# Attention ahead of a Sinkhorn-routed MoE on one core: another order of TensorE's pieces in the attention

## The chip, the cores and the metric

One Trainium2 chip, one of its cores. The metric is device time in microseconds of one execution of the whole program, which is attention followed by a mixture of experts. Of several executions the median is given.

Names of engines: PE is TensorE (matmuls and transposes), DVE is VectorE, ACT is ScalarE, POOL is GpSimd, SP is SyncE, which only issues DMAs here. PSUM is the memory that PE writes its results to, in banks of 128 partitions by 512 fp32 columns. SBUF is the memory for everything else.

## The reference

```python
def _attn_ref(q, k, v, M_prev, z_prev, beta):      # B, H, S, D = 4, 8, 576, 64
    scores = scale * np.matmul(q, k.transpose(0, 1, 3, 2))
    scores = np.where(causal, -1000000000.0, scores)
    a = np.exp(scores - scores.max(-1, keepdims=True))
    a /= a.sum(-1, keepdims=True) + 1e-09
    local = np.matmul(a, v)
    q_p = np.where(q > 0, q, np.exp(q) - 1.0) + 1.0          # phi(q), the feature map
    mem_ret = np.einsum('bhsd,bhde->bhse', q_p, M_prev)
    mem_norm = np.einsum('bhsd,bhd->bhs', q_p, z_prev)[..., None] + 1e-06
    g = 1.0 / (1.0 + np.exp(-beta))[None, :, None, None]
    return g * mem_ret / mem_norm + (1 - g) * local
...
def _moe_ref(x, w_gate, w1, w2):                   # N, D, E, F = 2304, 512, 8, 1024
    logits = x @ w_gate
    P = np.exp(logits - logits.max())
    for _ in range(8):                             # Sinkhorn
        P /= P.sum(1, keepdims=True) + 1e-09
        P /= P.sum(0, keepdims=True) + 1e-09
        P *= N / E
    for e in range(E):
        out += P[:, e:e + 1] * (np.maximum(x @ w1[e], 0.0) @ w2[e])
```

The attention's output, with heads side by side, is the x of the experts.

## The kernel before

The attention works on 16 **pairs** p, each two heads of one batch. Its work takes about the first 275 us of the program. The experts fill the rest, and the change does not touch them.

For one pair the function `attention` (it is printed below) has these pieces. Each is a Python function that issues instructions on several engines:

- `load`: q, k, v, z and M of the pair from DRAM, by SP.
- `qkt`: ten transposes of q and k on PE into three PSUM tiles. Each tile is split into a high part on ACT (L230) and a low part on DVE (L231, tiles ql and kl). A tile is free again when both have read it.
- `phi_`: the feature map. ACT takes exp(q) (L256), DVE clips it (L257) and adds it to max(q, 0) (L258), POOL multiplies by z (L261, L265). `nrm` sums that on DVE (L274, L277), adds 1e-6, takes the reciprocal and scales it by the gate (L278 to L280). `pv_in` scales v on POOL (L286).
- `scores`: the matmuls of q and k (L303), in three passes of high and low parts. The call for row tiles 3 and 2 comes first, that for 1 and 0 later. DVE masks the result and takes the row's extreme value (L317), ACT the exponential (L324). `scores_tail` does the same for the last 64 rows of both heads (L335, L341, L347).
- `t_a`: 14 transposes of the exponentials of row tiles 3 and 2 into four PSUM tiles (L361), copied to SBUF by ACT and DVE (L362, L367) into eB and e3, which exist once. `t_b`: the 11 transposes of the others, in three tiles (L379 to L404).
- `r_stats`: DVE makes the reciprocals of the row sums (L415 to L417), POOL scales phi by them (L420, L425).
- `r_trans`: transposes of the reciprocals and of phi (L433, L434, L455) into two tiles. The reciprocals go by DVE (L436) and two DMAs to a DRAM buffer rd, and by two more DMAs to rsb, spread over the partitions.
- `pv` 0 and 1: the product with v, and that with M, for the first 256 and the other 320 rows of the sequence (L470, L475, L481), each followed by a copy on ACT (L487).
- `comb` 0 and 1: POOL multiplies the result x by rsb (L494) and splits it into xh and xl for the experts (L497, L498).

Pieces of the experts' first work are set among them from pair 5 on: `logits_a` and `logits_b` (L535, L549), and `first_parts` for the first chunk of each batch, matmuls into the bank f (12 at L621 or 6 at L636, with copies at L645).

The order is set so. Each piece has a **phase**, a number in the list `atoms` (L502 to L509). The pieces of all pairs are sorted by p plus phase, and are called in that order. On PE the instructions stand exactly as called: `manual_schedule` with PE as its only engine fixes that. On the other engines the program that builds the kernel chooses the order of instructions; each engine then runs its own list strictly from first to last. The transposes, the scores, `logits_a` and `logits_b` all take PSUM tiles from one pool `s` of six banks in turn: a tile must wait until the sixth tile before it has been read. x and f have one bank each. The tile `tmp` of the feature map, eA, eB, e1, e3, e4 and qn4 exist once; phi, rr, rm, vs, rsb, xc exist twice.

Of the kernel before, what the change touches and what calls it, by code (L numbers as in the profile page):

```python
# [17 lines left out]
def kernel(  # L18
# [78 lines left out]
    def f32(ap):  # L97
        return ap.bitcast(F32)
# [72 lines left out]
    def attention():  # L171
        with ExitStack() as actx:
# [286 lines left out]
            def pv(p, grp):  # L459
                w = GB if grp else GA  # L460
                x = ps.tile([128, 512], F32, tag="x", name="x", bufs=1)
                vs, qp = st[p]["vs"], st[p]["qp"]
                parts = (
                    [(kt, lambda h, kt=kt: eB[:, h, kt], 0, GB) for kt in range(3)]
                    + [(3, lambda h: e3[:, h], 128, GB), (4, lambda h: e4t[:, h], 256, GB)]
                    if grp else [(0, lambda h: eA[:, h], 0, GA), (1, lambda h: e1[:, h], 128, GA)]
                )
                for kt, ee, c0, c1 in parts:
                    for h in range(2):
                        nc.tensor.matmul(  # L470
                            out=x[half[h], c0:c1], lhsT=vs[:, kt, h], rhs=ee(h),
                            start=(kt == 0), stop=False,
                        )
                for h in range(2):
                    nc.tensor.matmul(  # L475
                        out=x[half[h], 0:256], lhsT=mraw[p % 3][:, half[h]],
                        rhs=qp[:, 256 * grp:256 * grp + 256], start=False, stop=(grp == 0),
                    )
                if grp:
                    for h in range(2):  # L480
                        nc.tensor.matmul(  # L481
                            out=x[half[h], 256:320], lhsT=mraw[p % 3][:, half[h]],
                            rhs=qp[:, 512 + 64 * h:576 + 64 * h], start=False, stop=True,
                        )
                xc = ap1.tile([128, GB], F32, tag="xc", name="xc", bufs=2)
                st[p]["xc", grp] = xc
                nc.scalar.copy(out=xc[:, 0:w], in_=x[:, 0:w])  # L487

            def comb(p, grp):
                b, hp = divmod(p, HP)  # L490
                c0, w = (0, GA) if grp == 0 else (GA, GB)
                cols = slice(b * S + c0, b * S + c0 + w)
                xc = st[p].pop(("xc", grp))
                nc.gpsimd.tensor_tensor(  # L494
                    out=xc[:, 0:w], in0=xc[:, 0:w], in1=st[p]["r"][:, c0:c0 + w], op=ALU.mult
                )
                nc.gpsimd.tensor_copy(out=xh[:, hp, cols], in_=xc[:, 0:w])  # L497
                nc.gpsimd.tensor_tensor(  # L498
                    out=xl[:, hp, cols], in0=xc[:, 0:w], in1=f32(xh[:, hp, cols]), op=ALU.subtract
                )  # L500
# [2 lines left out]
                (-1.6, load), (-0.40, qkt), (-0.38, phi_), (-0.36, pv_in), (-0.10, nrm),  # L503
                (0.00, lambda p: scores(p, (3,))), (0.01, lambda p: scores(p, (2,))),
                (0.30, lambda p: scores(p, (1, 0))), (0.31, scores_tail),
                (0.50, t_a), (0.80, t_b), (0.70, r_stats), (0.90, r_trans),
                (0.95, lambda p: pv(p, 0)), (1.15, lambda p: pv(p, 1)),
                (1.45, lambda p: comb(p, 0)), (1.46, lambda p: comb(p, 1)),
            ]  # L509
            seq = [  # L510
                (p + ph, lambda f=f, p=p: f(p)) for p in range(NPAIR) for ph, f in atoms
# [434 lines left out]

    setup()
    attention()
    front.close()
    experts()  # L950
# [30 lines left out]
```

## Time and profile before

| what | value |
|---|---|
| time before, median of 3 runs | 1772.59 us |
| lowest and highest run | 1772.06 and 1774.39 us |
| span of the profiled execution, first to last instruction | 1770.6 us |
| mean granted TensorE clock over the span | 0.996 |
| PE busy over the span | 97% |
| DVE, POOL, ACT busy over the span | 73%, 66%, 39% |

The profile gives the profiled execution by its span alone; the median of the timed runs is 2.0 us longer than that span. A share of busy time is an average over the attention, in which all four compute engines work in a chain, and the experts, in which PE hardly ever stops. So the attention has to be read by itself, in stretches of one pair. As the mark of a pair the text takes the start of L455, the four transposes of phi in `r_trans`.

### The profile page before, as it was taken

The page shows a single profiled execution, that of the slowest core. Times are in us where ns is not written, and L with a number is a line of the kernel's source. Part 1 is how long each engine was busy: PE and PEld are TensorE (multiplying, and loading weights), DVE is VectorE, ACT ScalarE, POOL GpSimd, SP SyncE. Part 2 cuts the span into 40 slices and gives each one's busy share as a digit, 9 for nine tenths or more (in the row PEclk, how much of TensorE's full clock was granted, in tenths as well). Part 3 has the DMA queues.
Part 4 walks back from the last instruction along what each step waited for, and adds up shares of the span by engine and source line. Part 5 has one row for each costly group of instructions (what it writes and reads, how often), then busy time and mean ns, then how long its engine had stood idle before and what let it go on. Part 6 is the DMA issues. An engine that isn't in the chain of part 4 may idle for free.

```text
span 1770.6 us, 26969 instructions
## 1 busy us (share of the span) xinstructions
PE 1723.7 (97%) x9381; PEld 1522.5 (86%) x9381; DVE 1289.0 (73%) x2371; ACT 685.7 (39%) x1550; POOL 1166.0 (66%) x1113
## 2 busy tenths in 40 slices
PE   5899999999999999999999999999999999999999
PEld 4677777889999999888899999998898999999998
DVE  6887873787777777767777777777667777777776
ACT  4766762233333333333333333333333333333332
POOL 4655543567777777676677777776676777777773
PEclk8999999999999999999999999999999999999999
DMA  4443414222222222214222222222142222222221
GB/s 109 105 103 96 114 41 149 57 70 71 72 66 61 65 72 72 72 49 142 72 71 61 65 66 72 72 72 72 48 143 72 65 61 66 72 72 72 72 60 48
DMA packets 154888, 135.55 MB, mean 77 GB/s; under 512 B 71424, under 2 KB 121728, under 8 KB 154752
## 3 DMA queue, kind: packets, MB, share of 16 engines
q1 hardware_dynamic: 154320, 133.05, 25.0%
q8 instruction: 74, 1.21, 0.3%
q10 hardware_dynamic: 432, 0.79, 0.1%
q14 instruction: 62, 0.51, 0.1%
HBM read 124.28 MB, written 9.51 MB: 76 GB/s over the span
## 4 chain that ended last, share of the span: by engine, by line
PE 81%; POOL 5%; DVE 4%; issue 4%; DMA 2%; ACT 2%; SPq 1%; POOLq 0%; ACTq 0%; DVEq 0%
PE s L636 40%; PE s L805 27%; PE f L805 9%; PE x L470 1%; ACT e L324 1%; DMA rsb<-rd 1%; PE s L303 1%; DVE hhl L790 1%; POOL tl L710 1%; POOL phi L425 1%; POOL w1l L756 1%; DVE acc L877 0%; PE s L621 0%; PE f L636 0%; POOL w2l L779 0%
## 5 line engine op out<-in xcount | busy, mean ns | idle before, releaser
L756 POOL TENSOR_TENSOR w1l<-raw,w1h 128x512 fp32r<-128x512 f32 x263 | 368.2, 1414 | 395.1 <-ACT w1h L755 394.9
L878 DVE SCALAR_TENSOR_TENSOR acc<-s,P,acc 128x512 f32<-128x512 f32 x504 | 369.2, 745 | 133.5 <-PE s L636 131.1
L636 PE MATMUL s<-w2h,hhh 128*128 128x512 f32 x1116 | 435.5, 390 | 6.0 <-DVE acc L878 5.9
L636 PE MATMUL s<-w2h,hhl 128*128 128x512 f32 x1116 | 436.1, 391 | 0.0
L636 PE MATMUL s<-w2l,hhh 128*128 128x512 f32 x1116 | 435.8, 391 | 0.0
L836 DVE TENSOR_TENSOR temps<-s,temps 128x384 f32<-128x384 f32 x447 | 242.5, 555 | 169.8 <-ACT w1h L755 83.0
L790 DVE SCALAR_TENSOR_TENSOR hhl<-temps,hhh 128x384 fp32r<-128x384 f32 x340 | 306.5, 901 | 0.0
L779 POOL TENSOR_TENSOR w2l<-raw,w2h 128x512 fp32r<-128x512 f32 x186 | 292.7, 1595 | 11.9 <-ACT w2h L778 11.9
L789 ACT ACTIVATE hhh<-temps 128x384 fp32r<-128x384 f32 x340 | 178.7, 526 | 297.8 <-DVE temps L836 289.9
L636 PEld LDWEIGHTS s<-w2h,hhh 128*128 128x128 f32 x1116 | 209.6, 188 | 50.6 <-DVE acc L878 9.5
L636 PEld LDWEIGHTS s<-w2h,hhl 128*128 128x128 f32 x1116 | 209.4, 188 | 44.0
L636 PEld LDWEIGHTS s<-w2l,hhh 128*128 128x128 f32 x1116 | 209.4, 188 | 41.5
L839 ACT COPY temps<-s 128x384 f32<-128x384 f32 x64 | 30.7, 480 | 413.7 <-PE s L805 412.6
L805 PE MATMUL s<-th,w1l 128*128 128x384 f32 x510 | 170.8, 335 | 1.5 <-POOL w1l L756 1.5
L805 PE MATMUL s<-tl,w1h 128*128 128x384 f32 x510 | 170.7, 335 | 0.8 <-POOL tl L710 0.8
L805 PE MATMUL s<-th,w1h 128*128 128x384 f32 x510 | 170.6, 334 | 0.0
L805 PE MATMUL s<-xh,w1l 128*128 128x384 f32 x480 | 161.7, 337 | 0.5 <-POOL w1l L751 0.5
L805 PE MATMUL s<-xh,w1h 128*128 128x384 f32 x480 | 161.7, 337 | 0.0
L805 PE MATMUL s<-xl,w1h 128*128 128x384 f32 x480 | 161.2, 336 | 0.0
L755 ACT CAST w1h<-raw 128x512 fp32r<-128x512 f32 x263 | 153.7, 615 | 3.7 <-issue 3.0
L836 DVE TENSOR_TENSOR temps<-f,temps 128x384 f32<-128x384 f32 x148 | 80.3, 555 | 55.3 <-PE f L805 26.2
L778 ACT CAST w2h<-raw 128x512 fp32r<-128x512 f32 x186 | 112.1, 607 | 0.0
(220 smaller groups left out, 2895.0 us busy)
## 6 DMA issues: line engine op xcount, KB each, us to landing
raw<-in_moe_w_dram SPq DMA_DIRECT2D x372, 256.0 KB
rsb<-rd SPq DMA_DIRECT2D x32, 144.0 KB
ydr<-wst SPq DMA_DIRECT2D x18, 256.0 KB
acc<-ydr SPq DMA_DIRECT2D x18, 256.0 KB
qraw<-in_q_dram SPq DMA_DIRECT2D x32, 128.0 KB
kraw<-in_k_dram SPq DMA_DIRECT2D x32, 128.0 KB
vraw<-in_v_dram SPq DMA_DIRECT2D x32, 128.0 KB
out_dram<-acc SPq DMA_DIRECT2D x15, 256.0 KB
```

Of the source, the lines that this page charges most:

```text
L303: nc.tensor.matmul(out=sp[h][:, at:at + w], lhsT=qq[x][half[h], 128 * i:128 * i + 128], rhs=kk[y][half[h], 0:w], start=(a == 0), stop=(a = ...
L636: nc.tensor.matmul(out=pt, lhsT=h_[:, f, cols], rhs=w[:, f], start=(n == 0), stop=(n == 5))
L755: nc.scalar.copy(out=wh[:, i:i + 2], in_=src)
L756: tt(out=wl[:, i:i + 2], in0=src, in1=f32(wh[:, i:i + 2]), op=ALU.subtract)
L778: nc.scalar.copy(out=wh[:, j], in_=raws[j])
L779: nc.gpsimd.tensor_tensor(out=wl[:, j], in0=raws[j], in1=f32(wh[:, j]), op=ALU.subtract)
L789: nc.scalar.activation(out=hh[:, f, c], in_=src, func=AF.Relu)
L790: late.append(lambda: nc.vector.scalar_tensor_tensor(out=hl[:, f, c], in0=src, scalar=0.0, in1=f32(hh[:, f, c]), op0=ALU.max, op1=ALU.subt ...
L805: nc.tensor.matmul(out=pt[:, 0:HT], lhsT=w[:, wi, k], rhs=x[:, k], start=(n == 0), stop=(n == total - 1),)
L836: nc.vector.tensor_tensor(out=o, in0=x, in1=y, op=ALU.add)
L839: nc.scalar.copy(out=X, in_=prod(q, [(0, b11)]))
L878: nc.vector.scalar_tensor_tensor(out=acc[:, j], in0=pt, scalar=P[:, t_, e:e + 1], in1=acc[:, j], op0=ALU.mult, op1=ALU.add,)
```

## The change

Six numbers in the list of phases. `t_a` goes from .50 to .65, `r_trans` from .90 to 1.02, `pv` 0 from .95 to 1.05, `pv` 1 from 1.15 to 1.35, and both halves of `comb` from 1.45 and 1.46 to 1.80 and 1.81. No instruction is added or taken away, and the experts' part of every engine's list is the same.

```diff
                 (-1.6, load), (-0.40, qkt), (-0.38, phi_), (-0.36, pv_in), (-0.10, nrm),
                 (0.00, lambda p: scores(p, (3,))), (0.01, lambda p: scores(p, (2,))),
                 (0.30, lambda p: scores(p, (1, 0))), (0.31, scores_tail),
-                (0.50, t_a), (0.80, t_b), (0.70, r_stats), (0.90, r_trans),
-                (0.95, lambda p: pv(p, 0)), (1.15, lambda p: pv(p, 1)),
-                (1.45, lambda p: comb(p, 0)), (1.46, lambda p: comb(p, 1)),
+                (0.65, t_a), (0.80, t_b), (0.70, r_stats), (1.02, r_trans),
+                (1.05, lambda p: pv(p, 0)), (1.35, lambda p: pv(p, 1)),
+                (1.80, lambda p: comb(p, 0)), (1.81, lambda p: comb(p, 1)),
```

**On PE.** The first place in PE's list where the two kernels part, just after the scores of pair 0. L361 is `t_a` of pair 0, L242 to L246 are the q and k transposes of pair 1, L379 to L399 are `t_b` of pair 0, and L303 at the end are the first scores of pair 1.

```order
-L361 MATMUL s<-ident,e 128x128 x14
 L242 MATMUL s<-ident,qraw_120 128x128 x4
 L242 MATMUL s<-ident,kraw_122 128x128 x4
 L245 MATMUL s<-ident,kraw_122 128x128
 L246 MATMUL s<-ident,qraw_120 128x128
+L361 MATMUL s<-ident,e 128x128 x14
 L379 MATMUL s<-ident,e 128x128 x4
 L388 MATMUL s<-ident,e 128x128 x2
 L389 MATMUL s<-ident,e_135 64x128
 L399 MATMUL s<-ident,e_135 128x128 x4
+L303 MATMUL s<-kh,qh 128x512 x2
+L303 MATMUL s<-kl,qh 128x512 x2
```

The 14 transposes of the exponentials now stand behind the next pair's q and k transposes, and the next pair's first scores stand ahead of `r_trans` (L433), which follows them. In the same way the second half of `pv`, which stood between those scores and the next ones, now stands behind the next pair's `scores_tail`, and with it behind the piece of the experts at x.33.

**On DVE.** A pair with an early piece of the experts, in DVE's list before: L436 and L452 are `r_trans` of one pair, L258 to L277 the feature map of the next pair and the sums over it, L317 the first scores of the next pair.

```order
L436 COPY rt<-s 9x128
L404 COPY e_133<-s 128x2x64
L452 COPY qp<-s 128x128
L258 SCALAR_TENSOR_TENSOR phi<-qraw_119,tmp 128x640
L274 TENSOR_REDUCE rm<-tmp 128x8
L277 TENSOR_REDUCE rm<-tmp 128x1
L317 ISA e,mn<-s,mask 128x512
L317 ISA mn 128x1
```

The same place in DVE's list of the changed kernel, from the last of the four L317 of the first scores on.

```order
L317 ISA e,mn<-s,mask 128x384
L317 ISA mn 128x1
L436 COPY rt<-s 9x128
L452 COPY qp<-s 128x128
L258 SCALAR_TENSOR_TENSOR phi<-qraw_119,tmp 128x640
L274 TENSOR_REDUCE rm<-tmp 128x8
L277 TENSOR_REDUCE rm<-tmp 128x1
L278 TENSOR_SCALAR rm<-rm 128x9
L279 RECIPROCAL rm<-rm 128x9
L280 TENSOR_TENSOR rm<-rm,gcol 128x9
L257 TENSOR_SCALAR tmp<-tmp 128x640
L317 ISA e,mn<-s,mask 128x256
```

The first scores now stand ahead of the feature map and of `r_trans`, and the feature map with all of `nrm` stands between the first scores and the next ones. Further down, still in the changed kernel, the low parts of q and k (L231) come straight behind the reciprocals.

```order
L645 COPY wst<-f 128x512
L415 TENSOR_SCALAR rr<-sum 128x9
L416 TENSOR_TENSOR rr<-rm,rr 128x9
L417 RECIPROCAL rr<-rr 128x9
L231 TENSOR_TENSOR ql<-s,qh 128x512
L231 TENSOR_TENSOR kl<-s,kh 128x512
L231 TENSOR_TENSOR kl<-s,kh 128x64
L367 COPY e_133<-s 128x128
L362 COPY eB<-s 128x3x128
```

Before, the copies of `t_a` (L362, L367) stood ahead of ql and kl; now they stand behind them.

**On POOL.** One pair in POOL's list before: L286 is `pv_in`, L494 to L498 both halves of `comb`, L420 and L425 the next pair's `r_stats`.

```order
L286 TENSOR_TENSOR vs<-vraw_123,ogb 128x640
L494 TENSOR_TENSOR xc<-xc,rsb 128x256
L494 TENSOR_TENSOR xc<-xc,rsb 128x320
L497 CAST xh<-xc 128x256
L497 CAST xh<-xc 128x320
L498 TENSOR_TENSOR xl<-xc,xh 128x256
L498 TENSOR_TENSOR xl<-xc,xh 128x320
L420 TENSOR_TENSOR qn_136<-phi,rr 64x64 x2
L425 TENSOR_TENSOR phi<-phi,rr 128x512
```

The same pair in POOL's list of the changed kernel.

```order
L494 TENSOR_TENSOR xc<-xc,rsb 128x256
L497 CAST xh<-xc 128x256
L498 TENSOR_TENSOR xl<-xc,xh 128x256
L420 TENSOR_TENSOR qn_136<-phi,rr 64x64 x2
L425 TENSOR_TENSOR phi<-phi,rr 128x512
L286 TENSOR_TENSOR vs<-vraw_123,ogb 128x640
L494 TENSOR_TENSOR xc<-xc,rsb 128x320
L497 CAST xh<-xc 128x320
L498 TENSOR_TENSOR xl<-xc,xh 128x320
L261 TENSOR_TENSOR tmp<-phi,zb_126 128x512
```

`comb` is now in two pieces: its first half still stands ahead of the next pair's `r_stats`, its second half behind, next to `pv_in` and straight ahead of the product L261 of the feature map.

## Rows read from the trace of the kernel before

**Rows 1.** Windows: window, length, busy us (instructions) of PE, PEld, DVE, ACT, POOL.

```profile
48.31:92.22 43.91, 39.00 (x333) 28.30 (x334) 39.36 (x128) 31.10 (x96) 29.82 (x40) 1.00 0.46 113
92.22:109.70 17.48, 17.48 (x135) 13.99 (x136) 13.49 (x44) 11.44 (x33) 8.68 (x12) 1.00 0.43 96
109.70:252.96 143.26, 139.45 (x1133) 108.41 (x1132) 117.28 (x397) 98.60 (x293) 79.01 (x108) 1.00 0.33 88
140.32:155.50 15.18, 14.83 (x126) 11.10 (x124) 12.30 (x46) 11.74 (x36) 8.78 (x12) 1.00 0.40 105
155.50:173.83 18.33, 17.66 (x135) 13.94 (x136) 13.71 (x44) 11.50 (x34) 8.69 (x12) 1.00 0.37 89
252.96:267.10 14.14, 13.70 (x116) 10.54 (x114) 9.72 (x37) 9.39 (x28) 5.57 (x9) 1.00 0.18 68
275.00:1770.00 1495.00, 1479.31 (x7429) 1335.37 (x7429) 1074.01 (x1650) 509.38 (x1027) 1019.27 (x907) 1.00 0.23 73
```

**Rows 2.** Waits summed, 100 to 268 us: total us, count, mean us.

```profile
POOL xc L494 <- DMA rsb<-rd: 24.2, 10, 7.5
...
DVE rm L274 <- POOL tmp L261: 12.6, 9, 1.4
```

**Rows 3.** DVE's timeline, pair 5 to 6: start us, duration us, idle before.

```profile
126.52 0.80 DVE L258 SCALAR_TENSOR_TENSOR phi<-qraw,tmp 128x640 f32<-128x640 f32 x1
128.73 0.69 DVE L274 TENSOR_REDUCE rm<-tmp 128x8 f32<-128x512 f32 x1 [1.41 <-POOL tmp L261]
...
129.53 0.68 DVE L317 CUSTOM_DVE_ANT_0 e<-s,mask 128x512 f32<-128x512 f32 x1
...
131.70 0.87 DVE L278 TENSOR_SCALAR rm<-rm 128x9 f32<-128x9 f32 x1
132.49 0.48 DVE L257 TENSOR_SCALAR tmp<-tmp 128x640 f32<-128x640 f32 x1
...
133.21 0.42 DVE L317 CUSTOM_DVE_ANT_0 e<-s,mask 128x256 f32<-128x256 f32 x1
...
134.32 0.45 DVE L341 CUSTOM_DVE_ANT_0 e<-s,mask 128x288 f32<-128x288 f32 x1
...
136.45 0.55 DVE L415 TENSOR_SCALAR rr<-sum 128x9 f32<-128x9 f32 x1 [0.39 <-ACT e L347]
...
138.38 0.64 DVE L231 TENSOR_TENSOR ql<-s,qh 128x512 fp32r<-128x512 f32 x1
```

**Rows 4.** ACT's timeline, the exponential of the feature map in that period.

```profile
129.64 0.74 ACT L256 ACTIVATE tmp<-qraw 128x640 f32<-128x640 f32 x1 [1.90 <-DMA kraw<-in_k_dram]
```

**Rows 5.** The chain of waits: two early pieces of the experts.

```profile
122.68 1.40 PE f L636 x6
...
233.94 2.81 PE f L621 x12
```

**Rows 6.** PE's timeline: end of the q and k transposes, start of t_b and of r_trans.

```profile
122.24 0.33 PE L245 MATMUL s<-ident,kraw 128*128 128x128 f32 x1 [0.80 <-ACT eB L362]
...
123.92 0.60 PE L379 MATMUL s<-ident,e 128*128 128x128 f32 x4
...
125.12 0.27 PE L433 MATMUL s<-ident,rr 128*9 128x128 f32 x1
```

**Rows 7.** PE's timeline, first pairs: `r_trans` of pair 0, scores of pair 1.

```profile
30.21 0.47 PE L434 MATMUL s<-ident,qn 128*128 128x128 f32 x1 [5.71 <-POOL qn L420]
...
34.71 0.80 PE L303 MATMUL s<-kh,qh 64*128 64x512 f32 x2
...
36.76 0.49 PE L470 MATMUL x<-eB,vs 128*64 128x320 f32 x2
```

**Rows 8.** POOL's timeline: `pv_in`, and the second half of `comb`.

```profile
130.98 1.56 POOL L286 TENSOR_TENSOR vs<-vraw,ogb 128x640 f32<-128x640 f32 x1 [1.87 <-PE x L470]
...
135.40 0.88 POOL L494 TENSOR_TENSOR xc<-xc,rsb 128x320 f32<-128x320 f32 x1
```

**Rows 9.** DVE's timeline, the same operation L278 near the start.

```profile
31.13 0.18 DVE L278 TENSOR_SCALAR rm<-rm 128x9 f32<-128x9 f32 x1
```

## The prediction

> **What bounds the kernel now.** I read the page first. It says that PE is busy 97% of the span, but over a program with two unlike halves that says little. So I went to the stretches between marks of pairs [rows 1]. Three things are to be seen there. The experts take 1495.00 us of the 1770.6 us span, with PE busy 1479.31 us. The change leaves that part of every engine's list as it is, so only the first 275 us can move, and 0.2% of the time (3.5 us, about what a measurement here can tell from no change) is 1.3% of the attention. Second, PE is idle 4.91 us in the three pairs to 92.22, nothing in the pair to 109.70, 3.81 us in the nine pairs to 252.96 and 0.44 us in the last. Third, the stretch to 109.70 has no idle PE and holds two early pieces of 12 matmuls. Each takes 2.81 us [rows 5], so a pair by itself costs PE 17.48 − 5.62 = 11.86 us, and one with two pieces of 1.40 us [rows 5] costs 14.66 us.
>
> The periods before are 14.64 us (43.91 / 3) without pieces, 15.18 us with logits and 18.33 us with two L621 pieces [rows 1], one stretch of two each. The nine pairs to 252.96 are two and two of these and five with two L636 pieces, so one of the five takes (143.26 − 2 × 15.18 − 2 × 18.33) / 5 = 15.25 us. PE could go faster in the first three kinds. So I looked at the waits and at DVE's timeline. DVE works its list strictly in order: for 39.36 of 43.91 us, or 13.1 us of each pair without pieces [rows 1]. It also stands still 1.4 us a pair at L274 for POOL's product L261 [rows 2]. At L415 it stands still for ACT's exponential of the tail, 0.39 us in the pair shown [rows 3]. 13.1 plus these waits is a period. In the pairs without early pieces DVE's queue sets the time and PE waits for it. With pieces the two are within 0.6 us of each other, and with L621 PE alone sets it.
>
> **The change part by part.** Nothing is added or taken away, so each edit is worth what its place is worth.
>
> *q, k transposes ahead of t_a, and what waits there now.* Before, the last tile of `qkt` waited 0.80 us for a copy of `t_a` [rows 6]. That wait goes. What is late next: the four tiles of `t_a` follow those of `qkt` in the six banks, and the last of them takes the bank that ql frees. In DVE's list ql now stands behind L415, L416 and L417. A new closed loop arises, around one period, from the first L317 of a pair to the first L317 of the next. With the rows of the pair 5 to 6 [rows 3, 4]:
>
> - four L317 of the first scores: 131.70 − 129.53 = 2.17
> - L436 and L452, two small copies, as estimate 0.2 each (L278, small too, takes 0.18 [rows 9]): 0.40
> - L258 to the start of L274, with L261 on POOL between: 128.73 − 126.52 = 2.21
> - start of L274 to the start of L256, which needs `tmp` free: 129.64 − 128.73 = 0.91
> - L256 on ACT 0.74, L257 on DVE 0.48; L278 to L280 fit beside L256 if each is as short as in rows 9
> - L317 of the later scores: 134.32 − 133.21 = 1.11
> - L341 to L415, with the wait for ACT: 136.45 − 134.32 = 2.13
> - L415 and two small operations, 0.55 + 2 × 0.18 = 0.91, then ql 0.64 [rows 3, 9]
> - PE: the last three transposes of `t_a`; eleven of `t_b` take 125.12 − 123.92 = 1.20 [rows 6], so three take 0.33; then L636 1.40 [rows 5], `t_b` 1.20
> - first scores up to what the first L317 needs, three passes over two heads: no more than six wide matmuls in a row, 1.40 [rows 5], and no less than half of that; I take 1.0, in the middle.
>
> Sum: 11.70 + 3.93 = 15.63 us. PE's own work would allow 14.66, the period was 15.25. Without the L636 piece the loop is 15.63 − 1.40 = 14.23 us; with L621 it would be 15.63 − 1.40 + 2.81 = 17.04 us, so PE's 17.48 stays the bound there.
>
> *Pairs 1 to 4, without pieces.* Loop 14.23, before 14.64: between −1.2 in all and nothing; POOL's list, below, speaks for the upper end, so 0. Bounds: DVE's pure work 13.1 gives −4.6; one more wait like L274's in two of the periods (2 × 1.4) gives +2.8.
>
> *Pair 4 to 5 (to 109.70).* PE has no idle time and the same work: 0, bounds ±0.3, a copy either way.
>
> *Pairs 5 to 14 (109.70 to 252.96).* Five L636 periods at 15.63, two logits periods as before at 15.18 (they bring one more tile from the six banks; ±1 each), two L621 periods at 17.5: 78.2 + 30.4 + 35.0 = 143.6, against 143.26: +0.3. Bounds: PE as the bound, −6.8 (5 × 0.59 + 2 × 1.08 + 2 × 0.85, where the logits' eight matmuls at 1.40 / 6 and four small transposes make some 2.2 us); above, half of the L274 wait added in each of nine periods, +6.3.
>
> *The last pair.* PE's 14.14 us [rows 1] held no next scores or transposes. I estimate those at 1.1 for `qkt` (ten transposes at 1.20 / 11 each) and first scores at 1.4, below the 36.76 − 34.71 = 2.05 that they take at the start [rows 7] and near six wide matmuls of L636. By 11.86 − 1.1 − 1.4 + 2.8 = 12.2 us PE could close it: −1.9. Bounds −2.5 and 0.
>
> *The start.* `r_trans` of pair 0 waited 5.71 us for POOL's qn [rows 7]. The first scores of pair 1, 2.05 us, stood behind that wait; now they stand ahead and are hidden by it: −2.05. `comb` of pair 0 no longer stands as a whole ahead of POOL's r_stats of pair 1, a second half of 0.88 for L494 [rows 8] and two operations more; of these I take 1.15, between nothing and some 2.5. Together −3.2; bounds −1.5 and −4.5.
>
> *`pv` 1 and `comb` later.* `pv` 1 is 2.7 us of the same PE work elsewhere. Its readers are ACT's L487 and `comb`, which the experts' pieces need only a pair later: nothing, while POOL keeps up. The two transfers through DRAM in `r_trans` start after the first scores, so rsb lands some 1.4 us later against its period; POOL's L494 waits for it anyway, 7.5 us on average [rows 2]. At the end of the attention the last `comb` goes through the same chain of rsb: 0, at most +0.5. SP issues the same DMAs; a load of z stands between them now, which is free while rsb has that slack (rival 3).
>
> Sum: −3.2 + 0 + 0 + 0.3 − 1.9 = −4.8 us on a span of 1770.6. The timed median is 2.0 us above that span, and I leave that distance as it is: 1772.6 − 4.8 = **1767.8 us**.
>
> **A rule weighed.** DVE's L278 works on nine columns. It took 0.18 us at 31.13 [rows 9], where POOL's instruction was just ending and none followed, and 0.87 us where it started inside POOL's L286 [rows 3, 8]. So something in POOL's two-input work holds DVE. The Trainium skill (SBUF — State Buffer, section "Who interferes with whom") says that DVE and GpSimd share one pair of ports, held exclusively, and that a DVE instruction with two SBUF inputs contends with GpSimd's reads. The trace agrees as far as L278's two times go. By that page L258, which has two SBUF inputs, would wait for a whole instruction of POOL; the sum above has it at its 0.80 us, and the difference is rival 2.
>
> **The rivals.**
>
> *1. PE becomes the bound.* If ql gets its turn early, as it may when DVE's L274 and L415 waits are covered by the new order, the loop opens. Then pairs without pieces take DVE's 13.1 (−4.6), the nine others go to −6.8, start and last pair as above: −16.5, 1756 us. For it: each link of the loop has slack if POOL's L261 starts earlier. Against it: the loop has L274's wait inside, and no operation of it is gone. Chance 0.2.
>
> *2. Slower: POOL's second half of `comb` holds DVE.* L494, L497 and L498 of 320 columns, with `pv_in` before them, now run ahead of L261 and beside L258 and `nrm`, which are in the loop. POOL's in-order list also puts them ahead of L261 itself. If L258 or L261 waits for just one such instruction of 0.88 us [rows 8] in each of the 13 periods from pair 1 to 14: +11.4, −4.8 + 11.4 = +6.6, 1779 us. It decides from (4.8 + 3.5) / 13 = 0.64 us a period on. Against it: POOL is busy only 79.01 of 143.26 us [rows 1], and its work can fall into DVE's scores. Chance 0.2.
>
> *3. rsb becomes late.* POOL's first half of `comb` stands ahead of r_stats, whose qn and phi PE's `r_trans` needs. If rsb lands 1.4 us later plus the z load's wait for POOL's L265, and POOL had less than that in hand, each period grows by some 0.4: 13 × 0.4 = +5.2, 1773 us. L494's wait of 7.5 us [rows 2] begins early because POOL has nothing else, so most of it is slack. Chance 0.1.
>
> **How the numbers follow.** The likeliest has 0.5, with a range of its own from 1763 to 1772 (the bounds of the start, the loop's 1.0 and the logits); just over six parts in ten of that lie more than 3.5 us below before. Rival 1 is faster throughout. Rival 2 is slower in three quarters of its range of prices, rival 3 in about half of its (0.4 is the middle of its prices, and it is slower by over 3.5 us from 0.64 on, as in rival 2). Faster: 0.31 + 0.20 = 0.51. Slower: 0.15 + 0.05 = 0.20. Within: 0.29. The range runs from 1757, which holds half of rival 1, to 1777.5, which leaves out the full price of rival 2.
>
> **What would show it.** In the profile after: no wait at L245, instead one of about a microsecond in PE's L361 for DVE's ql; L636 periods of 15.6 us and logits periods of 15.2; qn's wait of 5.71 shrunk by some 2 us and the mark of pair 1 (48.31 before) near 45; the last period near 12.2. Rival 1 would show as PE without idle time and periods of 14.7. Rival 2 would show as L258 of well over 0.8 us, or L274 waiting longer than 1.4 us for L261 with L498 just ahead of that on POOL. Rival 3: PE's L434 waiting for POOL behind L494. The prediction fails most easily at the loop's PE part, if the banks' turns are other than I read them, and at the pairs without pieces, where half a microsecond in each is as large as the whole sum of the nine later ones.

## The result and the profile after

| kernel | median us (lowest to highest) | ratio to before, 95% interval |
|---|---|---|
| before, beside the changed kernel | 1773.49 (1772.06 to 1775.50) | |
| changed | 1797.66 (1793.58 to 1800.68) | 1.0132 [1.0113, 1.0151] |

The changed kernel is 24 us slower, outside the predicted range and on the other side of before. The profiled execution has a span of 1798.6 us, 28.0 us more than that of before. The windows between the marks of pairs (starts of L455), with the columns of [rows 1] and then the granted clock, the DMA share and GB/s:

```profile
45.63:94.26 48.63, 40.28 (x335) 30.22 (x334) 38.42 (x130) 32.20 (x96) 30.45 (x42) 0.93 0.44 109
94.26:115.55 21.29, 19.31 (x138) 15.24 (x137) 12.68 (x47) 12.22 (x34) 9.53 (x13) 0.92 0.34 79
115.55:278.94 163.39, 145.65 (x1133) 112.22 (x1132) 111.93 (x398) 102.29 (x293) 79.26 (x108) 0.96 0.29 78
278.94:294.77 15.83, 13.85 (x103) 10.91 (x102) 7.81 (x31) 8.56 (x26) 5.71 (x9) 0.89 0.11 37
303.00:1798.00 1495.00, 1478.02 (x7421) 1334.05 (x7420) 1072.94 (x1648) 509.10 (x1026) 1017.91 (x906) 1.00 0.24 73
```

They are pairs 1 to 4, 4 to 5, 5 to 14, the last, and the experts. The experts are as before: 1478.02 us of PE work in 1495 us, against 1479.31 us [rows 1]. All of the loss lies in the attention: +4.7, +3.8, +20.1 and +1.7 us in these four stretches, and only the start gained (the mark of pair 1 came at 45.63 in place of 48.31, −2.7). That sums to +27.7 of the 28.0. PE stands idle far more than before: 17.74 us of 163.39, against 3.81 of 143.26. The last column but two shows a second thing: the granted clock, 1.00 in every one of the stretches of [rows 1], is below that here.

The waits summed from 45 to 300 us (total us, count, longest us) say where PE stands:

```profile
POOL xc L494 <- DMA rsb<-rd: 58.4, 11, 6.5
...
PE x L475 <- ACT qp L456: 28.9, 14, 3.0
DVE ql L231 <- ACT qh L230: 23.0, 11, 2.9
DVE rm L274 <- POOL tmp L261: 17.9, 13, 1.4
...
PE s L361 <- DVE ql L231: 1.1, 1, 1.1
```

The row that decides is L475, the product with M in `pv` 0. It waits in 14 pairs for qp, which L456 copies on ACT out of the transposes of phi. Before, no such wait stood in the sums. The other large rows are waits of POOL and DVE, and cost nothing while PE is late. PE's timeline and then ACT's, pair 7 to 8:

```profile
150.99 0.60 PE L455 MATMUL s<-ident,phi 128*128 128x128 f32 x4
151.52 0.65 PE L470 MATMUL x<-eA,vs 128*64 128x256 f32 x4
152.01 0.39 PE L470 MATMUL x<-e,vs 128*64 128x128 f32 x4
154.34 0.65 PE L475 MATMUL x<-qp,mraw 128*64 128x256 f32 x4 [1.95 <-ACT qp L456]
154.93 0.39 PE L303 MATMUL s<-kh,qh 64*128 64x256 f32 x2
```

```profile
151.10 0.73 ACT L324 ACTIVATE e<-e,mn 128x512 f32<-128x512 f32 x1 [1.15 <-DVE mn L317]
...
151.83 0.71 ACT L324 ACTIVATE e<-e,mn 128x512 f32<-128x512 f32 x1
...
152.53 0.60 ACT L324 ACTIVATE e<-e,mn 128x384 f32<-128x384 f32 x1
...
153.13 0.60 ACT L324 ACTIVATE e<-e,mn 128x384 f32<-128x384 f32 x1
...
153.73 0.56 ACT L456 COPY qp<-s 128x512 f32<-128x512 f32 x1
155.12 0.37 ACT L487 COPY xc<-x 128x256 f32<-128x256 f32 x1 [0.83 <-POOL tmp L261]
```

The transposes of phi are done at 151.6. ACT begins its first exponential of the scores that were moved ahead at 151.10 and works its list in order: four L324, 2.63 us together, and only then L456. PE gets qp at 154.3 and stands for 1.95 us. Every later instruction of PE's fixed list stands behind it. In the kernel before, L456 followed the copies of `t_b` on ACT (L400 is the last of them), ahead of these exponentials:

```profile
125.41 0.51 ACT L400 COPY eB<-s 128x384 f32<-128x384 f32 x1
125.97 0.59 ACT L456 COPY qp<-s 128x512 f32<-128x512 f32 x1
...
130.31 0.72 ACT L324 ACTIVATE e<-e,mn 128x512 f32<-128x512 f32 x1
```

The clock, in windows of one microsecond around the same wait behind the mark at 115.55 (columns as above), and PE's row there:

```profile
116.00:117.00 1.00, 0.95 (x10) 0.48 (x8) 1.00 (x5) 1.00 (x3) 0.00 (x0) 1.00 0.00 0
117.00:118.00 1.00, 0.00 (x0) 0.00 (x0) 1.00 (x5) 1.00 (x5) 0.00 (x0) 1.00 0.00 0
118.00:119.00 1.00, 0.08 (x2) 0.08 (x4) 0.27 (x1) 0.87 (x3) 0.65 (x1) 1.00 0.02 4
119.00:120.00 1.00, 1.00 (x6) 0.25 (x6) 0.35 (x1) 0.00 (x0) 1.00 (x2) 0.51 0.00 1
...
121.00:122.00 1.00, 1.00 (x8) 0.88 (x7) 0.84 (x3) 0.30 (x1) 0.00 (x0) 0.50 0.15 41
122.00:123.00 1.00, 1.00 (x7) 0.96 (x7) 1.00 (x9) 0.74 (x3) 0.00 (x0) 0.78 0.35 101
123.00:124.00 1.00, 1.00 (x6) 0.73 (x4) 0.84 (x4) 1.00 (x6) 0.00 (x0) 1.00 0.80 208
```

```profile
118.92 1.06 PE L475 MATMUL x<-qp,mraw 128*64 128x256 f32 x4 [1.97 <-ACT qp L456]
```

PE stood for 1.97 us. Then the granted clock is 0.50 (1.2 of 2.4 GHz) for over three microseconds, and the same four matmuls that took 0.65 us at full clock in the pair above take 1.06. Two L636 pairs of this kernel with the same wait, one with such a fall (115.55 to 134.00) and one without (134.00 to 150.99), last 18.45 and 16.99 us: the fall costs 1.5 us. From 45 us to the end of the attention the trace has seven falls, each behind one of the fourteen waits. In the attention of the profiled execution of before there is none after 36 us.

### The profile page after: what moved, and what is told of

Read it like the earlier page. It is cut to its first block, busy times and chain, and to the rows that moved or that the text cites. A ratio compares the mean times of both kernels' runs of the same rounds, so it can differ in the third digit from the quotient of the medians.

```text
span 1798.6 us, 26911 instructions
## 1 busy us (share of the span) xinstructions
PE 1735.4 (96%) x9381; PEld 1531.0 (85%) x9381; DVE 1279.3 (71%) x2371; ACT 691.4 (38%) x1550; POOL 1166.1 (65%) x1113
## 4 chain that ended last, share of the span: by engine, by line
PE 85%; DVE 4%; POOL 3%; issue 3%; ACT 3%; SPq 1%; DMA 1%; POOLq 0%; ACTq 0%; DVEq 0%
PE s L636 39%; PE s L805 27%; PE f L805 9%; ACT e L324 2%; PE x L470 2%; PE s L303 1%; PE s L361 1%; PE f L636 1%; PE f L621 1%; PE x L475 1%; PE s L335 1%; DVE hhl L790 1%; POOL tl L710 1%; PE s L242 1%; POOL w1l L756 1%
## 5 line engine op out<-in xcount | busy, mean ns | idle before, releaser
L636 PE MATMUL s<-w2h,hhh 128*128 128x512 f32 x1116 | 435.4, 390 | 5.7 <-DVE acc L878 5.6
L636 PE MATMUL s<-w2h,hhl 128*128 128x512 f32 x1116 | 436.2, 391 | 0.0
L636 PE MATMUL s<-w2l,hhh 128*128 128x512 f32 x1116 | 435.8, 391 | 0.0
L636 PEld LDWEIGHTS s<-w2h,hhh 128*128 128x128 f32 x1116 | 209.5, 188 | 50.2 <-DVE acc L878 9.2
L636 PEld LDWEIGHTS s<-w2h,hhl 128*128 128x128 f32 x1116 | 209.4, 188 | 44.0
L636 PEld LDWEIGHTS s<-w2l,hhh 128*128 128x128 f32 x1116 | 209.4, 188 | 41.5
```

Of the source, the lines that this page charges most:

```text
L636: nc.tensor.matmul(out=pt, lhsT=h_[:, f, cols], rhs=w[:, f], start=(n == 0), stop=(n == 5))
```

## The experiments

The theory after the result, **A**: L456's place on ACT, behind the exponentials that were moved ahead of `r_trans`, makes PE stand some 2 us a pair, and a part of these stalls costs the clock as well. The rivals: **B**, the q and k transposes ahead of `t_a`; **C**, `pv` 1 and `comb` late; later **D**, the loop through DVE that the prediction summed.

### r_trans alone moved back ahead of the scores

```diff
-                (0.65, t_a), (0.80, t_b), (0.70, r_stats), (1.02, r_trans),
+                (0.65, t_a), (0.80, t_b), (0.70, r_stats), (0.995, r_trans),
```

> The changed kernel with r_trans at .995 in place of 1.02: its transposes stand ahead of the next pair's first scores again, all else as changed. Theory A (ACT's list: the copy L456 of phi's transposes stands behind the four exponentials L324 of the scores that were moved ahead, PE's L475 waits 14 times some 2.0 us for it, and after a part of these stalls the granted clock falls to 0.5): L475 waits under 0.3 us, the clock stays at 1.00 from 50 us on, 28.9 us and all of the clock's loss go, 1757 to 1770 us. Rival B (the q and k transposes ahead of t_a, with ql waiting for ACT's copy qh, 23.0 us in all): still above 1785. Rival C (pv 1 and comb late): still above 1785.

Measured: 1760.39 us, ratio 0.9928 [0.9913, 0.9943]. One piece put 0.025 of a phase earlier takes 37 us off the changed kernel, and makes it 13 us faster than before. The wait at L475 is gone. The windows of its marks, pairs 1 to 4, 4 to 5, 5 to 14 and the last:

```profile
46.99:88.66 41.67, 38.40 (x336) 28.89 (x334) 37.31 (x131) 32.66 (x99) 31.63 (x41) 1.00 0.46 111
88.66:106.17 17.51, 17.51 (x135) 13.95 (x136) 11.82 (x42) 11.58 (x33) 11.41 (x15) 1.00 0.45 106
106.17:242.82 136.65, 136.65 (x1134) 108.32 (x1132) 112.12 (x397) 101.00 (x293) 80.07 (x109) 1.00 0.36 95
242.82:256.39 13.57, 13.57 (x116) 10.54 (x115) 8.74 (x34) 8.87 (x27) 5.58 (x10) 1.00 0.17 63
```

From 88.66 to 256.39 us PE is not idle at all, at full clock. The L636 periods are 14.66 us, the logits periods 14.22, the L621 periods 17.46. These are PE's own work, as the prediction's first part has it. ACT and DVE of this kernel, where the changed one had its wait:

```profile
135.53 0.48 ACT L400 COPY eB<-s 128x384 f32<-128x384 f32 x1
136.13 0.59 ACT L456 COPY qp<-s 128x512 f32<-128x512 f32 x1
138.13 0.72 ACT L324 ACTIVATE e<-e,mn 128x512 f32<-128x512 f32 x1 [1.41 <-DVE mn L317]
```

```profile
136.44 0.98 DVE L258 SCALAR_TENSOR_TENSOR phi<-qraw,tmp 128x640 f32<-128x640 f32 x1
137.34 0.68 DVE L317 CUSTOM_DVE_ANT_0 e<-s,mask 128x512 f32<-128x512 f32 x1
...
139.52 0.68 DVE L274 TENSOR_REDUCE rm<-tmp 128x8 f32<-128x512 f32 x1
```

L456 is ahead of the exponentials. And DVE's list has changed with it: L258 now stands ahead of the four L317, L274 behind them, so POOL's product L261 between the two is hidden and L274 hardly waits any more (1.5 us in all). So this run undoes two things, the place of L456 and the order L258, L274 on DVE. The next runs show what the first of the two is worth.

### r_trans late, alone on the kernel before

```diff
-                (0.50, t_a), (0.80, t_b), (0.70, r_stats), (0.90, r_trans),
-                (0.95, lambda p: pv(p, 0)), (1.15, lambda p: pv(p, 1)),
+                (0.50, t_a), (0.80, t_b), (0.70, r_stats), (1.02, r_trans),
+                (1.05, lambda p: pv(p, 0)), (1.15, lambda p: pv(p, 1)),
```

> The kernel before with r_trans at 1.02 and pv 0 at 1.05 alone, t_a, pv 1 and comb at their old places. Theory A: L456 stands behind the exponentials here too, L475 waits some 2 us in most of 14 pairs, and the time rises to 1788 to 1802 us. Rivals B and C: the parts that they blame are absent, 1768 to 1777 us.

Measured: 1811.11 us, 1.0216 [1.0198, 1.0234]. PE's waits, 45 to 300 us:

```profile
PE x L475 <- ACT qp L456: 27.0, 14, 2.0
PE x L470 <- ACT xc L487: 7.4, 14, 0.6
```

The one step makes the same wait in 14 pairs without the parts that B and C blame. It is worse than expected: `pv` 1 here follows at once and waits for ACT again, for the copy L487 that frees the bank x (7.4 us), and the clock falls eight times from 45 us on. How the loss divides between the two was not measured.

### The copy L456 on DVE, PE's list unchanged

```diff
-                nc.scalar.copy(out=qp[:, 0:512], in_=t_)
+                nc.vector.tensor_copy(out=qp[:, 0:512], in_=t_)
```

> The changed kernel with the copy L456 on DVE in place of ACT; PE's list is the same. In DVE's list it stands behind the four L317 of the same scores, L436 and L452, so by the changed trace it could end at some 153.6 in place of 154.3 (pair 7). Theory A: the wait at L475 falls from 1.95 to some 1.2 us and is released by DVE, 14 times 0.75 is 10 us, and fewer falls of the clock give up to 10 more: 1778 to 1787 us. Rivals B and C: DVE has more to do and nothing else changes, 1797 to 1808 us.

Measured: 1784.58 us, 1.0062 [1.0047, 1.0077]. The expectation of A was 1.2 us a wait and 1778 to 1787 us:

```profile
PE x L475 <- DVE qp L456: 17.9, 15, 1.3
PE s L361 <- DVE ql L231: 5.9, 3, 2.0
```

Fifteen waits of 1.2 us, now released by DVE. PE's list is that of the changed kernel to the last instruction, and 13 us are gone, so the places of the pieces that B and C blame can't be all of the loss. One thing that B names did change: ql's wait for qh fell from 23.0 to 9.1 us, as ACT has a copy less. But in the changed kernel PE itself waited for ql only once from 45 us on. The second row is new: three times in the pairs without early pieces PE waits 1.9 us for ql, and behind each of these waits, at 60, 77 and 94 us, the clock falls.

### The product with M behind the next scores

The four L475 of `pv` 0 and the copy behind them become a function `pv_m`, called at a phase of its own:

```diff
-                (1.05, lambda p: pv(p, 0)), (1.35, lambda p: pv(p, 1)),
+                (1.05, lambda p: pv(p, 0)), (1.305, lambda p: pv_m(p, 0)), (1.35, lambda p: pv(p, 1)),
```

> The changed kernel with the four L475 of pv 0 (the product with M) and the copy behind them taken out of pv 0 and called at 1.305, so that the later scores of rows 1 and 0 (0.83 us of PE) stand ahead of them. L456 keeps its place on ACT behind the exponentials. Theory A: the wait falls by those 0.83 us to 1.1 us, 14 times 0.83 is 12 us, and the clock falls more seldom (up to 10 us more): 1774 to 1786 us. Rivals B and C: 1795 to 1800 us.

Measured: 1779.05 us, 1.0035 [1.0025, 1.0045]. L484 is the old L475 in this file:

```profile
PE x L484 <- ACT qp L456: 16.9, 14, 1.8
```

The wait fell to 1.2 us, as PE had 0.83 us of work ahead of it. Five L636 periods last 16.1 to 16.3 us. With these waits the clock stayed at 1.00 from 56 us on. Two doses of the wait, made smaller on PE's side and on the copy's side, agree: an L636 period without a fall is 14.66 us of work, plus the wait, plus some 0.3.

The same at 1.312, behind `scores_tail`:

```diff
-                (1.05, lambda p: pv(p, 0)), (1.35, lambda p: pv(p, 1)),
+                (1.05, lambda p: pv(p, 0)), (1.312, lambda p: pv_m(p, 0)), (1.35, lambda p: pv(p, 1)),
```

> The changed kernel with the product with M of pv 0 and the copy behind it called at 1.312, behind scores_tail: PE has 1.75 us of work ahead of it. L456 stays behind the exponentials on ACT, and DVE's list keeps L258 and L274 between the two sets of scores. Theory A: the wait for L456 is under 0.4 us; the copy of x on ACT now stands behind more exponentials, so pv 1 may wait up to 1 us for the bank x in pairs without an early piece; L636 periods of 14.7 to 15.2, 1763 to 1773 us. Rival D (the loop through DVE that the prediction summed to 15.63 us): L636 periods of 15.5 us or more with no wait for L456, 1771 to 1777 us.

Measured: 1792.93 us, 1.0106 [1.0088, 1.0125]. A's first half held, its time did not:

```profile
PE x L470 <- ACT xc L496: 22.9, 13, 3.4
PE x L484 <- ACT qp L456: 2.2, 12, 0.4
```

The wait for L456 is 0.2 us each. But the copy of x (L496 here) fell behind the next four exponentials on ACT, and `pv` 1 waits for the bank x, 1.8 us each. It is the same loss at the next place. It tells nothing on D, since these periods (17.2 us) are longer than D's loop.

### r_trans and pv 0 both back at their old places

```diff
-                (0.65, t_a), (0.80, t_b), (0.70, r_stats), (1.02, r_trans),
-                (1.05, lambda p: pv(p, 0)), (1.35, lambda p: pv(p, 1)),
+                (0.65, t_a), (0.80, t_b), (0.70, r_stats), (0.9, r_trans),
+                (0.95, lambda p: pv(p, 0)), (1.35, lambda p: pv(p, 1)),
```

> The changed kernel with r_trans at .90 and pv 0 at .95, both where they were before; t_a, pv 1 and comb as changed. ACT's list has L456 ahead of the exponentials. Theory A (L456's place on ACT is all of the loss): no wait of 2 us at L475, no fall of the clock after 50 us, 1757 to 1766 us, like the kernel with r_trans at .995. Rival E (it is the scores between r_trans and pv 0 that made that kernel fast, by covering L456's copy and the start): some 0.5 us of wait at L475 in each pair, 1765 to 1772 us.

Measured: 1773.63 us, 1.0000 [0.9989, 1.0011]. Both expectations missed. Two of PE's waits and one of DVE's:

```profile
PE s L335 <- DVE mn L317: 8.6, 10, 1.3
PE s L361 <- DVE ql L231: 5.2, 3, 2.2
...
DVE rm L274 <- POOL tmp L261: 14.1, 10, 1.4
```

The wait for L456 is gone, as A says, and so are 24 us. But all scores now follow one another on PE, and the tiles of the tail wait for banks that DVE's L317 has yet to read. The L636 periods are 15.6 and 16.1 us. And DVE's list has L274 straight behind L258 again, ahead of the scores, as before: L274 waits 1.4 us for L261 in ten pairs. So 24 of the 37 us go when L456 stands ahead of the exponentials, though L274 still waits. The other 13 go with two things that differ between this kernel and the one at .995, `pv` 0 between the two sets of scores and the place of L274; which of them is worth how much is not shown.

### t_a late, alone on the kernel before

```diff
-                (0.50, t_a), (0.80, t_b), (0.70, r_stats), (0.90, r_trans),
+                (0.65, t_a), (0.80, t_b), (0.70, r_stats), (0.9, r_trans),
```

> The kernel before with t_a at .65 alone. Theory F (the gain of 13 us with r_trans at .995 comes from t_a behind the q and k transposes, which takes away the waits at L245 and L433, 5.8 us in all, and what follows from them): 1760 to 1768 us. Rival G (it comes from pv 1 behind scores_tail, which gives PE 2.7 us of work while the exponentials are made): 1770 to 1778 us, with new waits at L361.

Measured: 1782.48 us, 1.0049 [1.0032, 1.0066], slower than either expected.

```profile
PE s L361 <- DVE ql L231: 12.0, 12, 1.9
```

This is the wait that the prediction put into the changed kernel, at the place and of the size that it gave: a microsecond a pair at L361 for ql. Here it is real. That it comes because `pv` 1 no longer stands ahead of `t_a` and gives DVE its time is likely, and not shown.

### With r_trans at .995, one of the other moves undone

```diff
-                (1.05, lambda p: pv(p, 0)), (1.35, lambda p: pv(p, 1)),
+                (1.05, lambda p: pv(p, 0)), (1.15, lambda p: pv(p, 1)),
```

> The kernel with r_trans at .995 and pv 1 back at 1.15, ahead of the later scores. Theory F: 1758 to 1763 us, L636 periods of 14.7. Rival G: 1767 to 1777 us, with waits of PE at the transposes of t_a for exponentials or at L470, and L636 periods of 15 or more.

Measured: 1806.50 us, 1.0183 [1.0163, 1.0203]: 46 us more than with `pv` 1 at 1.35, far beyond G's 1767 to 1777, at another place than G named first.

```profile
PE x L470 <- ACT xc L487: 31.4, 14, 2.4
```

The two halves of `pv` share the bank x. With the second straight behind the first, it waits 2.2 us a pair for the copy L487, which ACT's list has behind four exponentials.

```diff
-                (0.65, t_a), (0.80, t_b), (0.70, r_stats), (0.995, r_trans),
+                (0.5, t_a), (0.80, t_b), (0.70, r_stats), (0.995, r_trans),
```

> The kernel with r_trans at .995 and t_a back at .50, ahead of the q and k transposes. If t_a's move is worth something by itself, the waits of L245 for a copy of t_a come back (0.7 us a pair), and perhaps waits of t_a for the exponentials: 1765 to 1775 us. If only pv 1's place counts: 1758 to 1763 us.

Measured: 1783.55 us, 1.0059 [1.0044, 1.0074]. `t_a`'s move is worth 23 us in this company. The expected waits at L245 hardly came (two in all, the longer 1.3 us); PE stood at L434 for qn and at L455 for phi instead, and some of its losses lie in stretches at the low clock (141 to 145, 196 to 199 and 230 to 233 us). What sets qn late there was not followed further.

```diff
-                (1.80, lambda p: comb(p, 0)), (1.81, lambda p: comb(p, 1)),
+                (1.45, lambda p: comb(p, 0)), (1.46, lambda p: comb(p, 1)),
```

> The kernel with r_trans at .995 and both halves of comb back at 1.45 and 1.46; the lists of PE, DVE and ACT are the same, only POOL's differs. Theory H (comb's later place is free, PE sets the time): 1758 to 1763 us, the periods of 14.66 stay. Rival I (the second half ahead of r_stats makes qn late): waits at L434 of some 0.5 us or more in each pair, 1765 to 1772 us.

Measured: 1763.60 us, 0.9947 [0.9928, 0.9966], beside 1760.39 in another comparison. H holds nearly: L434 has no waits from 45 us on, and two of the five L636 periods are 15.1 and 15.2 us instead of 14.66; the two intervals overlap. On the changed kernel itself the same edit gave:

> The changed kernel with both halves of comb back at 1.45 and 1.46, other lists the same. Theory A: the waits at L475 stay at 28 us, 1792 to 1801 us. Rival C (comb late): 1775 to 1785 us.

Measured: 1794.33 us, 1.0116 [1.0099, 1.0133], with 25.6 us of waits at L475 in 13 pairs. C falls: `comb`'s place is worth some 3 us at most, with opposite signs in the two kernels, and in both the intervals overlap.

## Why the prediction was wrong, step by step

**The step that failed** is the one that the prediction never priced. It followed the first scores ahead of `r_trans` on PE ("now they stand ahead and are hidden"), on DVE and on POOL, and asked of each what is queued behind what. It did not ask that of ACT. There the four exponentials of those scores, 2.6 us, came to stand ahead of L456, for which PE's L475 waits. That row is not in the sum, not in the bounds, and no rival has it. It measured 28.9 us of stalls in the profiled execution.

**A second cost had no term either.** Seven of the stalls were followed by a stretch at half clock. Against the kernel with `r_trans` at .995, whose span is 1757.8 us, the changed one has 40.8 us more: 28.9 of waits, and 11.9 that I put down to seven falls of the clock at 1.5 us and more each. That they fit together is a sum, not a separate experiment, and a rough one: it leaves out the 0.3 us beside each wait, the 1.4 us by which the changed kernel was ahead at the mark of pair 1, and the idle time of the other kernel in its first pairs. That both go when the wait goes is shown; two runs show that waits of 1.1 to 1.3 us left the clock alone. What decides after which of the equal waits the clock falls stays open: the waits at 118.92 and 137.39 are of 1.97 and 1.99 us, and only the first was followed by a fall.

**The start** came out near: −3.2 forecast, −2.7 measured at the mark of pair 1. Its parts did not come as summed: PE's wait for qn fell from 5.71 to 0.64 us, not by some 2, and a new wait of 2.54 us stands at `t_a`'s L361 ahead of it. That the total fits is in part luck.

**Pair 1 to 4** (0 forecast, +4.7), **4 to 5** (0, +3.8), **5 to 14** (+0.3, +20.1) and **the last** (−1.9, +1.7) were all missed by that one wait and the falls of the clock behind it. With `r_trans` at .995 they are −2.2, 0.0, −6.6 and −0.6 against [rows 1]: PE's 17.5 in the L621 pair was right, and PE's floor of 14.66 in the L636 pair, too. The −1.9 of the last pair was too large even there.

**The loop of 15.63 us** did not bind in the changed kernel, where its mark, the wait at L361 for ql, comes twice in the whole attention. That the stalls at L475 give DVE the time is likely, and not shown. The sum also lacks a link on ACT: it has ql straight behind L417, but DVE stood 23.0 us in 11 waits at ql for ACT's copy qh. The loop is not refuted in general: with `t_a` late alone the wait comes 12 times, 1.0 us each, in L636 periods of 15.7 to 16.6 us, but for one with a fall of the clock. In the kernel with `r_trans` at .995 DVE's list is another, and the loop's links of L258, L261 and L274 lie beside the scores.

**The rivals.** Rival 1, PE as the bound with periods of 14.7 and 1756 us, is what the kernel with `r_trans` at .995 comes near, 1760.4 us, with L274 moved on DVE as well. With the wait gone but L274 where it was before, the time was 1773.6 us, so what the changed kernel would do without the wait alone stays open. Rival 2 did not come: L258 took 0.80 us, with POOL idle each time, and L274 waited 1.4 us for L261 as before. Rival 3 did not come: L494 waited longer for rsb (58.4 us in all, against 31.7 before), and PE's L434 did not wait for POOL from 45 us on.

**The rule on shared ports** was weighed for rival 2. In the kernel before, L278 took 0.74 to 1.47 us in 13 of 16 pairs. Each time POOL's L286 was running when it began, and it ended with it (at 132.57 and 132.54 us in the pair of [rows 3, 8]). In the changed kernel it took 0.17 us at 139.03 us, where POOL had just stopped. L258 did not run beside POOL before or in the changed kernel, but it did in the kernel with `r_trans` at .995: 1.17 us where it began 0.49 us before POOL's L498 ended, 0.80 us where POOL was idle. So both wait for about what is left of a running POOL operation. For L258 that was 0.37 us at most, against the 0.88 of rival 2. These times agree with what the Trainium skill states (SBUF — State Buffer, section "Who interferes with whom"). The part on two SBUF inputs, which the prediction drew on, is seen in L258; L278 has one. What the shorter L278 is worth in time was not tested.

## What to carry to other kernels

When an order on one engine is changed, every other engine's list is to be read for what moved ahead of what, copies above all: here a 0.6 us copy on ACT behind 2.6 us of exponentials that PE did not yet need cost more than all the gains of the change. Moves of this kind do not add: `t_a` late alone cost 9 us, `r_trans` late alone 38 us, and all moves together, but with `r_trans` just ahead of the scores, gained 13 us. So a table of phases is tried whole, with the one piece shifted that the trace names.

## What the runs showed of the hardware

The granted clock fell from 1.00 to 0.50 after stalls of PE of some 2 us in the middle of a busy stretch, and came back 3.4 us later, with PE at work (119.0 to 122.4 us); one fall, from 262.4 to 269.2, lasted twice as long. A stall of 2 us so cost some 3.5 us where the clock fell (18.45 against 16.99 us of two like pairs, beside the 2 us that both have), and once 4.9 (19.93 against 16.99).

Not every such stall was followed by a fall: seven of the fourteen in the changed kernel were not, and with the product with M at 1.312 the clock stayed at 1.00 from 96 us on, through five waits of 1.8 us. The two kernels with stalls of 1.1 to 1.3 us had four falls, at 52, 60, 77 and 94 us, and each followed a longer wait, of 1.8 to 2.0 us; behind the shorter ones none came.
